# Moving the widening of weights out of the last attention slots into the first MLP

## The chip, the core and the metric

One core of a Trainium2 chip runs the whole program. Its engines are TensorE (PE, matmuls), VectorE (DVE), ScalarE (ACT), GpSimd (POOL) and SyncE (SP), which here only issues DMAs. The metric is the device time of one execution in microseconds (us), lower is better. Times inside the trace count from the first instruction.

## What is computed

Attention with random features, then an MLP block that mixes tokens and channels, then a block with a Fourier transform, a normalisation and a wider MLP. All in float32, for 4 x 576 tokens of 512 features.

```python
def _attn_ref(q, k, v, omega):
    ...
    q_p, k_p = (phi(q_s), phi(k_s))          # exp(proj - |x|^2/2 - max) / sqrt(m)
    kv = np.einsum('bhsm,bhsd->bhmd', k_p, v)
    z = np.sum(k_p, axis=2)
    num = np.einsum('bhsm,bhmd->bhsd', q_p, kv)
    den = np.einsum('bhsm,bhm->bhs', q_p, z)[..., None] + 1e-06
    return (num / den)

def _moe_ref(x, w_tok1, w_tok2, w_ch1, w_ch2):
    xt = x.transpose(0, 2, 1)
    h = np.maximum(xt @ w_tok1, 0.0) @ w_tok2
    u = x + h.transpose(0, 2, 1)
    h2 = np.maximum(u @ w_ch1, 0.0) @ w_ch2
    return (u + h2)

def _moe2_ref(x, w_ch1, w_ch2):
    ...                                       # u = x + real(fft2(x)), un = normalised u
    ch = np.maximum(un @ w_ch1, 0.0) @ w_ch2
    return (u + ch)
```

## The kernel before

Every matmul is made of three: a float32 operand is split into a high part that TensorE multiplies exactly and a low rest, and high x high, high x low and low x high are summed. The activations are split on the fly. The weights come to the core as 64-bit words and are **widened** there into a high and a low part. One chunk of weights (a slab of the first MLP, or half a pair of the second) takes one load, seven steps on VectorE, one on ScalarE and one store back to DRAM (the tile `kept`, 1 MB); when a matmul needs it, SP fetches it from there into a slot in SBUF.

The steps of a chunk of 1024 columns are, in order, with the weight that the planner gives them in us: take (L341, 0.68), ScalarE's scale (L348), rest (L352, 0.68), size (L356, 0.69), high (L360, 1.21), low (L364, 1.21), unit (L368, 0.69), scaled (L372, 1.22). After L364 the load of the chunk after next is issued (L330), after L372 the store (L406 for a slab). In attention loads and stores go through SP's queue, four steps after they fall due; from the end of attention on (`side.defer, side.queue = 0, pool`) they go through POOL's, at once.

`Side` holds the steps in one list. Its `step(budget)` is called at fixed places of the program; it adds the budget to a credit, and takes steps from the list as long as the credit covers them. So the budgets set at which place of VectorE's order a step stands, and nothing waits for a clock.

Attention runs in 72 slots and a tail of 7 (numbers n from 0 to 78). A slot projects four heads of a tile of 128 keys or queries (L506), makes its features (maximum L520, difference L527 and exponential L524 or L528), three slots later adds a key's features into the sums (L540, copied out at L545) or transposes a query's (L565), and five slots later divides (L582, L595 to L602). Keys and queries alternate; the last slot of a key is n = 60, and from there to 71 the slots are queries. Once a batch's rows are done, its token mix is put on the list `fill`, of which a slot takes about one: L667 for the hidden part, L680 for the way back, which VectorE adds into the residual (L683). Those of the last batch are still on the list when attention ends.

The first MLP (`ch_block`) runs over five blocks of the columns, the second of them short (256 columns). A block goes through the 12 slabs, the first block upwards, the second downwards. An iteration makes the hidden part of slab i (`up`, 12 matmuls, L776), takes its positive part and splits it (ScalarE L860, VectorE L861), multiplies slab i-1 down into four banks (`down`, L898), takes one item of `fill`, and calls `side.step`. The first `up` is already made in attention's tail. A slab that isn't stored yet can't be fetched: SP's instruction for it (L738) waits for the store to land, and all fetches behind it in SP's queue wait with it.

Before the change the budgets are 0 for n < 6, 1.2 up to 9, 0.45 up to 35 and 1.2 for the rest of attention, 3.9 in the first block, 1.2 in the second, and 4.3 in the others.

Of the kernel before, what the change touches and what calls it, by code (L numbers as in the profile page):

```python
# [32 lines left out]

SLOT0_US, SLOT1_US, SLOT_US, FIRST_US, SHORT_US, CH_US, FF_US, S_US, SAVED_US = 1.2, 0.45, 1.2, 3.9, 1.2, 4.3, 3.8, 1.6, 4.6


NP = NFF // 2
# [152 lines left out]
def pieces(t0, n):  # L192

    done = 0
    while done < n:
        b, s = divmod(t0 + done, S)
        step = min(n - done, S - s)
        yield done, step, b, s
        done += step
# [103 lines left out]
def mix_kernel(ctx: ExitStack, tc: tile.TileContext, qt, kt, va, om, w1, w2, wch, wff, t1, t2, out):  # L303
# [230 lines left out]
    def kv_add(i, g, part):  # L534

        off, n, b, s = part
        if s == 0:
            kvp[b, g] = bank("H")
        for hh in range(4):
            pe.matmul(out=kvp[b, g][:, hh * 65:hh * 65 + 65], lhsT=ft["k", i, g][:, hh, :],  # L540
                      rhs=src["v", i, int(off > 0)][:, 4 * g + hh, :], start=(s == 0 and hh == 0), stop=(s + n == S),
                      skip_group_check=True)
        if s + n == S:
            t = e0.tile([128, 4, D + 1], F32, tag=f"kvs{g}", name="kvs", bufs=2)
            dve.tensor_copy(out=t.rearrange("p h d -> p (h d)"), in_=kvp[b, g][:, 0:260])  # L545
            kvs[b, g] = t
            if (b, g) == (B - 1, 1):
                spare.extend("AAH")
# [12 lines left out]
    def turn(i, g):  # L561
        tp = bank("S")
        f = ft.pop(("q", i, g))
        for hh in range(4):
            pe.transpose(tp[:, hh * 128:hh * 128 + 128], f[:, hh, :], ident)  # L565
        qpt[i, g] = []
        for off, n, b, _ in pieces(i * 128, 128):
            if n < 128:
                act.copy(out=mixed_q[g][:, :, 2 * off:2 * off + n],
                         in_=tp.rearrange("p (a b) -> p a b", a=4)[:, :, off:off + n])  # L570
                t = mixed_q[g][:, :, off:off + 128]
            else:
                t = e0.tile([128, 4, 128], F32, tag="qpT", name="qpT", bufs=3)
                act.copy(out=t.rearrange("p a b -> p (a b)"), in_=tp)
            qpt[i, g].append((b, t))
# [112 lines left out]
    def last_tile(b):  # L688
        return ((b + 1) * S - 1) // 128

    order = [("k", i, g) for i in range(last_tile(0) + 1) for g in range(2)]
# [14 lines left out]
    side = Side()  # L706
# [74 lines left out]
    def attention():  # L781
        tiles = [(kind, i) for kind, i, g in order if g == (kind == "q")]
        at = {t: order.index(t + (int(t[0] == "q"),)) for t in tiles}
        late = {}
        n_all = len(order)

        def at_slot(n, kind):
            return order[n][1:] if 0 <= n < n_all and order[n][0] == kind else None

        def sums(n):  # L790
            if n in late:
                late.pop(n)()
            if (t := at_slot(n - LAG, "k")) is not None:
                parts = list(pieces(t[0] * 128, 128))
                kv_add(*t, parts[0])
                if len(parts) > 1:
                    late[n + 2] = lambda: kv_add(*t, parts[1])

        def queries(n):
            if (t := at_slot(n - LAG, "q")) is not None:  # L800
                turn(*t)
            t = at_slot(n - LAG_X, "q")
            if t is not None and t[1] == 0:
                turn_x(t[0])
                for b in range(B):
                    if t[0] == last_tile(b):
                        fill.extend(tok_mix(b))

        def results(n):
            if (t := at_slot(n - LAG_NUM, "q")) is not None:  # L810
                numer(*t)
                divide(*t)
                if t[1] == 0:
                    split_x(t[0])

        loads, splits = list(tiles), list(tiles)
        for n in range(-1, n_all + LAG_X):
            while loads and at[loads[0]] <= n + AHEAD_LOAD:
                load(*loads.pop(0))
            if n == n_all:  # L820
                enter_mlp()
            if 0 <= n < n_all:
                project(*order[n])
            sums(n)
            queries(n)
            while splits and at[splits[0]] <= n + AHEAD_SPLIT:
                split_in(*splits.pop(0))
            if 0 <= n < n_all:
                feature(*order[n])
            results(n)  # L830
            if n >= 2:

                side.step(0.0 if n < 6 else SLOT0_US if n < 10 else SLOT1_US if n < 36 else SLOT_US)
            if fill and (len(fill) > 3 or n % 2 == 0):
                fill.pop(0)()
            for fn in early[:3]:
                fn()
            del early[:3]
# [759 lines left out]
```

## Time and profile before

| | |
|---|---|
| Time, median of 3 runs | 955.7 us (954.63 to 956.05) |
| The profiled execution | 956.15 us, its span 954.1 us |
| TensorE busy | 934.5 us (98%), mean granted clock 0.996 |
| VectorE busy | 644.6 us (68%) |
| ScalarE busy | 301.5 us (32%) |
| POOL busy | 118.4 us (12%) |

Busy means that at least one instruction is under way. The granted clock is the share of TensorE's full 2.4 GHz; 0.50 is 1.2 GHz. Attention takes about the first 215 us, the first MLP's first block goes on to 291, the second block to 325.

### The profile page before, as it was taken

Reading aid. Unit: us, or ns where it says so; the run is one execution under the profiler, and the core shown is the slowest. Engines: PE = TensorE matmul, PEld = TensorE weight load, DVE = VectorE, ACT = ScalarE, POOL = GpSimd, SP = SyncE. Lnnn points to the kernel's source line nnn. Section 1 sums busy time; section 2 is a strip of 40 time slices with the busy share of each in tenths; the row PEclk is TensorE's granted clock in tenths of the full one; section 3 lists DMA queues with packets and bytes.
Section 4 is the critical chain, followed back from the end, with each engine's and each line's share of the span. In section 5 each row is a group of like instructions: output and inputs, shape, how many; then the busy total and the mean of one; then the engine's idle time right before and its main releaser. Section 6 shows DMA issues by size and latency. Waiting matters only on the chain.

```text
span 954.1 us, 14058 instructions
## 1 busy us (share of the span) xinstructions
PE 934.5 (98%) x5344; PEld 831.3 (87%) x5344; DVE 644.6 (68%) x1270; ACT 301.5 (32%) x676; POOL 118.4 (12%) x110
## 2 busy tenths in 40 slices
PE   7999999999999999999999999999999999999998
PEld 7999898888889988888888888889999998899986
DVE  5997989987776687877864577667565458533342
ACT  5886666651222222221221212222311113311121
POOL 3343333221121122011000000000000000000000
PEclk9999999899999999999999999999999999999999
DMA  7764454379999386585146438739777756787764
GB/s 267 230 198 163 147 213 167 129 300 323 348 349 424 116 325 224 193 284 194 43 179 214 161 131 272 259 113 359 268 244 242 231 183 219 227 263 256 251 208 157
DMA packets 68257, 216.47 MB, mean 227 GB/s; under 512 B 5600, under 2 KB 14432, under 8 KB 54240
## 3 DMA queue, kind: packets, MB, share of 16 engines
q1 hardware_dynamic: 60992, 172.40, 52.3%
q0 software_dynamic: 7056, 43.06, 12.3%
q8 instruction: 42, 0.69, 0.3%
q14 instruction: 23, 0.19, 0.1%
q10 hardware_dynamic: 144, 0.13, 0.0%
HBM read 169.30 MB, written 42.47 MB: 222 GB/s over the span
## 4 chain that ended last, share of the span: by engine, by line
PE 89%; DVE 8%; ACT 1%; issue 1%; DMA 0%; DVEq 0%; ACTq 0%
PE H L776 23%; PE A L898 16%; PE A L1470 14%; PE H L1457 12%; PE A L1264 7%; PE A L506 4%; PE N L582 2%; PE A L667 2%; PE H L540 2%; DVE mx L520 1%; PE S L1077 1%; DVE cvo L364 1%; PE S L1090 1%; PE S L680 1%; PE A L565 1%; DVE x L598 1%
## 5 line engine op out<-in xcount | busy, mean ns | idle before, releaser
L776 PE MATMUL H<-uh,w 128*128 128x512 f32 (+1 forms) x800 | 215.1, 354 | 1.5 <-ACT x L621 1.5
L776 PEld LDWEIGHTS H<-uh,w 128*128 128x128 f32 x800 | 136.4, 189 | 21.7 <-ACT x L621 1.7
L860 ACT ACTIVATE hh<-H 128x512 fp32r<-128x512 f32 (+1 forms) x92 | 49.0, 533 | 267.3 <-PE H L776 267.1
L776 PE MATMUL H<-ul,w 128*128 128x512 f32 (+1 forms) x304 | 113.4, 373 | 0.0
L898 PE MATMUL A<-hh,w 128*128 128x512 f32 (+1 forms) x480 | 108.7, 369 | 0.0
L1470 PE MATMUL A<-w2t,b 128*128 128x512 f32 x384 | 99.2, 394 | 0.0
L861 DVE SCALAR_TENSOR_TENSOR hl<-H,hh 128x512 fp32r<-128x512 f32 (+1 forms) x92 | 55.8, 607 | 64.0 <-ACT hh L860 63.8
L898 PEld LDWEIGHTS A<-hh,w 128*128 128x128 f32 x480 | 84.2, 188 | 15.1
L1457 PE MATMUL H<-b,w1t 128*128 128x384 f32 x480 | 91.5, 336 | 0.0
L1457 PEld LDWEIGHTS H<-b,w1t 128*128 128x128 f32 x480 | 85.0, 188 | 4.0 <-DVE tmp L1501 0.3
L1470 PEld LDWEIGHTS A<-w2t,b 128*128 128x128 f32 x384 | 70.6, 188 | 11.8
L524 ACT ACTIVATE f<-A,mx 128x128 f32<-128x128 f32 x200 | 57.5, 390 | 28.1 <-DVE mx L520 24.0
L776 PEld LDWEIGHTS H<-ul,w 128*128 128x128 f32 x304 | 57.3, 188 | 9.1
L898 PE MATMUL A<-hl,w 128*128 128x512 f32 (+1 forms) x240 | 59.2, 368 | 0.0
L1264 PE MATMUL A<-w,hh 128*128 128x512 f32 x192 | 50.5, 395 | 0.0
L520 DVE TENSOR_REDUCE mx<-A 128x4 f32<-128x512 f32 x71 | 48.2, 682 | 2.7 <-PE A L506 2.1
L898 PEld LDWEIGHTS A<-hl,w 128*128 128x128 f32 x240 | 42.6, 188 | 7.6
L364 DVE SCALAR_TENSOR_TENSOR cvo<-cvo,stg 128x1024 f32<-128x1024 int32 (+2 forms) x32 | 41.1, 1283 | 0.0
L540 PE MATMUL H<-v,f 128*128 128x65 f32 x320 | 40.1, 270 | 0.9 <-ACT f L524 0.9
L540 PEld LDWEIGHTS H<-v,f 128*128 128x128 f32 x320 | 38.9, 191 | 1.3 <-ACT f L524 1.1
L1264 PEld LDWEIGHTS A<-w,hh 128*128 128x128 f32 x192 | 34.6, 189 | 6.1
L1462 ACT ACTIVATE b<-tmp 128x384 fp32r<-128x384 f32 x16 | 8.4, 525 | 98.1 <-DVE tmp L1523 98.1
(253 smaller groups left out, 1705.1 us busy)
## 6 DMA issues: line engine op xcount, KB each, us to landing
w<-kept SPq DMA_DIRECT2D x60, 1024.0 KB, 6.9
w2t<-kept SPq DMA_DIRECT2D x55, 512.0 KB, 5.0
w1t<-kept SPq DMA_DIRECT2D x48, 512.0 KB, 4.9
stg<-in_wff_dram POOLq DMA_DIRECT2D x16, 1024.0 KB, 6.9
kept<-cvo POOLq DMA_DIRECT2D x13, 1024.0 KB, 7.4
stg<-in_wch_dram SPq DMA_DIRECT2D x9, 1024.0 KB, 6.0
kept<-cvo POOLq DMA_DIRECT2D x16, 512.0 KB, 7.6
kept<-so SPq DMA_DIRECT2D x16, 512.0 KB, 7.5
```

The costliest lines, as they stand in the source:

```text
L364: dve.scalar_tensor_tensor(out=st["l"].bitcast(F32), in0=st["l"], scalar=2.0 ** 32, in1=st["lw"].bitcast(U32), op0=ALU.mult, op1=ALU.add)
L506: pe.matmul(out=pj[:, p_ * 256:p_ * 256 + 256], lhsT=a[:, c, :], rhs=w, start=(n == 0), stop=(n == 2), skip_group_check=True)
L520: dve.tensor_reduce(out=mx, in_=p4, axis=AX.X, op=ALU.max, negate=True)
L524: act.activation(out=f[:, hh], in_=p4[:, hh], func=AF.Exp, bias=mx[:, hh])
L540: pe.matmul(out=kvp[b, g][:, hh * 65:hh * 65 + 65], lhsT=ft["k", i, g][:, hh, :], rhs=src["v", i, int(off > 0)][:, 4 * g + hh, :], start=( ...
L776: pe.matmul(out=hb[:, 0:n], lhsT=w(a, kk), rhs=u[:, kk, 0:n], start=(c == 0), stop=(c == 11))
L860: act.activation(out=hh, in_=hb[:, 0:n], func=AF.Relu)
L861: dve.scalar_tensor_tensor(out=hl, in0=hb[:, 0:n], scalar=0.0, in1=hh, op0=ALU.max, op1=ALU.subtract)
L898: pe.matmul(out=acc[i][:, 0:cols], lhsT=a[:, cs], rhs=v, start=(n == 0 and c_ == 0), stop=(n == NCH - 1 and c_ == 2))
L1264: pe.matmul(out=acc[t], lhsT=a[:, t * 128:t * 128 + 128], rhs=w, start=(n == 0 and c_ == 0), stop=(n == NFF - 1 and c_ == 2))
L1457: pe.matmul(out=to, lhsT=w[:, a, cs], rhs=v[:, q], start=(start and n == 0), stop=(n == 5), skip_group_check=True)
L1470: pe.matmul(out=acc[t], lhsT=h[n // 2][:, t * 128:t * 128 + 128], rhs=w[:, n % 2], start=(begins and n == 0), stop=(ends and n == 2))
```

## The change

Four budgets get other numbers, and a fifth is new: ALONE_US = 0.3, for the ten slots n = 58 to 67 (`alone` is the slot after the last key's, 61). The slots from 10 to 35 go from 0.45 to 0.5, the other slots from 36 on from 1.2 to 1.15. The first block's budget goes from 3.9 to 4.3, the second's from 1.2 to 1.7.

```diff
-SLOT0_US, SLOT1_US, SLOT_US, FIRST_US, SHORT_US, CH_US, FF_US, S_US, SAVED_US = 1.2, 0.45, 1.2, 3.9, 1.2, 4.3, 3.8, 1.6, 4.6
+SLOT0_US, SLOT1_US, SLOT_US, ALONE_US, FIRST_US, SHORT_US, CH_US, FF_US, S_US, SAVED_US = 1.2, 0.5, 1.15, 0.3, 4.3, 1.7, 4.3, 3.8, 1.6, 4.6
...
+        alone = max(n for n, x in enumerate(order) if x[0] == "k") + 1
...
-                side.step(0.0 if n < 6 else SLOT0_US if n < 10 else SLOT1_US if n < 36 else SLOT_US)
+                side.step(0.0 if n < 6 else SLOT0_US if n < 10 else SLOT1_US if n < 36 else
+                          ALONE_US if alone - 3 <= n < alone + 7 else SLOT_US)
```

What it moves stands in the order of the instructions on VectorE; TensorE's are in the same order as before. The lines below L835 have moved down by two in the new kernel (L861 is L863).

VectorE before, behind the last key's slot (x_1192 is a batch's residual, kvs the sums over the keys, mx and df the features' maximum and difference, rd the reciprocal in the division; cvo, cvy and stg belong to the widening):

```order
L372 SCALAR_TENSOR_TENSOR cvo<-cvo,cvy 128x1024
L352 TENSOR_SCALAR cvo<-stg 128x1024
L683 TENSOR_TENSOR x_1192<-A,x_1192 128x288
L545 COPY kvs<-H 128x260
L520 TENSOR_REDUCE mx<-A 128x4
L356 TENSOR_SCALAR cvo<-cvy 128x1024
L520 TENSOR_REDUCE mx<-A 128x4
L527 TENSOR_TENSOR df<-A,mx 128x512
```

VectorE after, at the same addition, copy and maxima (the residual is called x_1196):

```order
L683 TENSOR_TENSOR x_1196<-A,x_1196 128x288
L545 COPY kvs<-H 128x260
L520 TENSOR_REDUCE mx<-A 128x4 x2
L527 TENSOR_TENSOR df<-A,mx 128x512
L595 TENSOR_SCALAR rd<-N 128x4
L596 RECIPROCAL rd<-rd 128x4
L598 TENSOR_TENSOR x<-N,rd 128x128 x2
L602 TENSOR_TENSOR x<-N,rd 128x2
L364 SCALAR_TENSOR_TENSOR cvo<-cvo,stg 128x1024
```

The widening steps ahead of the addition and between the maxima are gone from here; the next one is a low (L364) behind a division.

VectorE before, in the first MLP block, from the second to the third of the eight additions of the last batch (x_2569 is its residual, hl the hidden part's low rest of the iteration):

```order
L683 TENSOR_TENSOR x_2569<-S,x_2569 128x288
L360 SCALAR_TENSOR_TENSOR cvo<-cvy,cvo 128x1024
L364 SCALAR_TENSOR_TENSOR cvo<-cvo,stg 128x1024
L368 TENSOR_SCALAR cvy<-cvo 128x1024
L341 TENSOR_SCALAR cvy<-stg 128x1024
L861 SCALAR_TENSOR_TENSOR hl<-H,hh 128x512
L683 TENSOR_TENSOR x_2569<-S,x_2569 128x288
L372 SCALAR_TENSOR_TENSOR cvo<-cvo,cvy 128x1024
```

VectorE after, in the same block, from the fourth to the fifth of the eight (the residual is called x_2552):

```order
L683 TENSOR_TENSOR x_2552<-S,x_2552 128x288
L352 TENSOR_SCALAR cvo<-stg 128x1024
L356 TENSOR_SCALAR cvo<-cvy 128x1024
L360 SCALAR_TENSOR_TENSOR cvo<-cvy,cvo 128x1024
L364 SCALAR_TENSOR_TENSOR cvo<-cvo,stg 128x1024
L368 TENSOR_SCALAR cvy<-cvo 128x1024
L863 SCALAR_TENSOR_TENSOR hl<-H,hh 128x512
L683 TENSOR_TENSOR x_2552<-S,x_2552 128x288
L341 TENSOR_SCALAR cvy<-stg 128x1024
L372 SCALAR_TENSOR_TENSOR cvo<-cvo,cvy 128x1024
```

The L372 that ends each of these two pieces is the last step of slab 11, the last slab of the first MLP: it stands behind the third addition before and behind the fifth after. The first MLP's block needs that slab in its twelfth iteration. Of the slabs' stores, six instead of five now go through POOL's queue in this block, and one fewer through SP's in attention.

## Rows read from the trace of the kernel before

**Rows 1.** The chain that ended last, share of the span by engine

```profile
PE 89%; DVE 8%; ACT 1%; issue 1%; DMA 0%; DVEq 0%; ACTq 0%
```

**Rows 2.** Stretches: length, busy us by engine (instructions), TensorE's granted clock, DMA

```profile
160.00:165.00 5.00, 4.22 (x36) 3.99 (x35) 4.90 (x12) 3.55 (x9) 1.34 (x2) 1.00 0.77 265
165.00:170.00 5.00, 3.01 (x24) 2.64 (x23) 5.00 (x7) 1.59 (x5) 2.17 (x1) 0.96 0.51 210
170.00:175.00 5.00, 4.70 (x22) 4.70 (x23) 4.83 (x11) 3.83 (x11) 2.37 (x1) 0.50 0.00 0
175.00:180.00 5.00, 5.00 (x40) 5.00 (x40) 4.43 (x12) 3.72 (x10) 2.57 (x2) 0.86 0.61 210
...
250.00:300.00 50.00, 50.00 (x274) 43.78 (x273) 36.47 (x53) 10.11 (x18) 9.45 (x11) 1.00 0.96 376
```

**Rows 3.** TensorE in order: start, us, instruction [idle before it and releaser]

```profile
153.27 0.36 PE L506 MATMUL A<-om_h,kh 128*128 128x256 f32 x1
...
168.14 0.54 PE L680 MATMUL A<-w2hl,h1h 128*128 128x288 f32 x2 [1.19 <-DVE x L683]
...
170.31 0.58 PE L506 MATMUL A<-om_h,qh 128*128 128x256 f32 x1 [1.10 <-ACT f L524]
```

**Rows 4.** VectorE in order, in attention, behind the last key's slot

```profile
164.00 2.04 DVE L372 SCALAR_TENSOR_TENSOR cvo<-cvo,cvy 128x1024 fp32r<-128x1024 f32 x1
165.97 1.75 DVE L352 TENSOR_SCALAR cvo<-stg 128x1024 int32<-128x1024 int32 x1
```

**Rows 5.** TensorE, first MLP block: the first matmul of up 9, 10, 11

```profile
269.68 0.39 PE L776 MATMUL H<-uh,w 128*128 128x512 f32 x1
...
275.92 0.40 PE L776 MATMUL H<-uh,w 128*128 128x512 f32 x1
...
282.17 0.39 PE L776 MATMUL H<-uh,w 128*128 128x512 f32 x1
```

**Rows 6.** VectorE in order, first MLP block

```profile
257.39 0.46 DVE L683 TENSOR_TENSOR x<-S,x 128x288 f32<-128x288 f32 x1 [1.72 <-PE S L680]
257.77 1.22 DVE L372 SCALAR_TENSOR_TENSOR cvo<-cvo,cvy 128x1024 fp32r<-128x1024 f32 x1
...
269.88 0.46 DVE L683 TENSOR_TENSOR x<-S,x 128x288 f32<-128x288 f32 x1 [1.72 <-PE S L680]
...
277.09 0.69 DVE L341 TENSOR_SCALAR cvy<-stg 128x1024 f32<-128x1024 f32 x1
```

**Rows 7.** POOL in order: stores of a slab

```profile
216.06 0.54 POOL L406 DMA_DIRECT2D kept<-cvo  x1 [0.76 <-DVE cvo L372]
...
259.28 1.03 POOL L406 DMA_DIRECT2D kept<-cvo  x1 [4.09 <-DVE cvo L372]
```

**Rows 8.** SP: a fetch, and its queue's waits from 256 to 268 (total, times, longest)

```profile
267.15 0.32 SPq L738 DMA_DIRECT2D w<-kept  x1
...
SPq L738 <- DMA kept<-cvo: 10.2, 1, 10.2
```

**Rows 9.** DMA landings (last column, us): fetches issued 211.13, 256.60, 267.15; stores 200.19, 248.00, 259.28

```profile
w<-kept SPq DMA_DIRECT2D x1, 1024.0 KB, 4.9
...
w<-kept SPq DMA_DIRECT2D x1, 1024.0 KB, 8.1
...
w<-kept SPq DMA_DIRECT2D x1, 1024.0 KB, 8.8
...
kept<-cvo SPq DMA_DIRECT2D x1, 1024.0 KB, 5.5
...
kept<-cvo POOLq DMA_DIRECT2D x1, 1024.0 KB, 6.9
...
kept<-cvo POOLq DMA_DIRECT2D x1, 1024.0 KB, 7.8
```

**Rows 10.** Second block: its last early fetch's landing, and that slab's first matmul

```profile
w<-kept SPq DMA_DIRECT2D x1, 1024.0 KB, 32.0
...
315.43 0.28 PE L776 MATMUL H<-uh,w 128*128 128x256 f32 x1
```

## The prediction

> **What bounds the kernel now.** I read the chain of waits first: 89% of the chain that ended last is TensorE and 8% VectorE [rows 1], so a change pays only where TensorE stands still, runs at its lower clock, or is made to. The table of stretches says where that is. In a stretch of 50 us from 250 on TensorE is busy for all 50 [rows 2]: after attention it never stands, and whatever delays it there is added to the time. Around the last key tile it does stand: of 5 us each it is idle for 0.78, 1.99 and 0.30 in the rows that begin at 160, 165 and 170, while VectorE is busy for 4.83 to 5.00. Its timeline names the waits: 1.19 us for the addition of a token-mix result (L683, VectorE), then 1.10 for the features (L524, which needs VectorE's maximum of L520) [rows 3]. The last projection of a key starts at 153.27 [rows 3]; from there the slots are queries alone, with less TensorE work in a slot, but a slot's share of widening is the same 1.2. VectorE's own rows there are widening steps, and two are stretched: L372 took 2.04 us and L352 took 1.75 [rows 4], where L372 takes 1.22 in the MLP [rows 6]. So VectorE sets the pace of these slots.
>
> The same rows show a second loss. After those idle stretches the granted clock fell: 0.96 of full in the row from 165, 0.50 (that is 1.2 instead of 2.4 GHz) in the row from 170, 0.86 in the row from 175. Lost to it: 5 x (0.04 + 0.50 + 0.14) = 3.4 us.
>
> **The change part by part.** TensorE's instructions stand in the same order in both kernels; only widening moves, on VectorE, with its DMAs and ScalarE's small step.
>
> *Ten slots at 0.3.* By the planner's weights the widening in slots 58 to 67 goes from 12.1 to 3.1, and the two stretched instructions leave. Slots 61 to 67 are then short of work on VectorE, not on TensorE. I book the idle time of three rows, 0.78 + 1.99 + 0.30 = 3.1 us, and the clock's 3.4 us, since the stand that came ahead of its fall is gone: **-6.5 us**. At worst the clock falls all the same or a chain from VectorE's maximum to ScalarE takes the place of the wait, and 3.1 or less is left. At best all of it goes, and that is what I book, since the chain has no third loss here that I could read. The three other slot numbers (0.45 to 0.5, 1.2 to 1.15) move 0.05 a slot: 26 slots up by 1.3 in all, 33 down by 1.7, where TensorE mostly runs; I book nothing, within 0.5 either way.
>
> *First block at 4.3, second at 1.7.* VectorE has room: in the MLP's first block an iteration lasts 6.2 us (starts at 269.68, 275.92 and 282.17 [rows 5]); one has a hidden part (L861, as many columns as L341 with its 0.69), an addition of 0.46 and widening of 3.3 to 4.5 by its weights, so 5.7 at most. The 4.4 and 5.5 more in the two blocks cost nothing by themselves as long as that room covers them.
>
> *What is late next: the slab's own way.* A slab that is widened in the block is stored by POOL, and SP's fetch waits for that store to land. With nine units less widened before the block, the rest comes later. The order on VectorE shows it for the last slab, 11: its last step L372 stood behind the third of the eight additions L683 of the last batch and now stands behind the fifth. Before: that addition at 257.39, L372 at 257.77 [rows 6], the store issued at 259.28 [rows 7], SP's fetch released by it at 267.15 after a wait of 10.2 us [rows 8], landing 8.8 us later [rows 9], at 275.95. It was needed at 282.17 [rows 5], so 6.2 us were spare (267.15 + 8.8 = 275.95). Two iterations later are 12.5 us, and the spare time is spent.
>
> After, in the times of this trace: fifth addition at 269.88 [rows 6] + 0.46, then L341 0.69 and L372 1.22 end at 272.25; the store follows 0.3 later (as 258.99 to 259.28), at 272.5. Stores beside a fetch took 6.9 and 7.8, fetches beside other transfers 8.1 and 8.8 [rows 9]. That gives 272.5 + 6.9 + 8.1 = 287.5 to 272.5 + 7.8 + 8.8 = 289.1. By the loneliest rows, a store of 5.5 and a fetch of 4.9 [rows 9], it would be 282.9. TensorE needs it at 282.17, so the stand is 5.3 to 6.9 us, and 0.7 at least. I take **+5.6 us**, near the lower row, because there is one load beside this fetch and no store until about 284, where the fetch of 8.8 had a load and two half stores beside it. Slab 10 is a smaller case of the same: its L372 now ends at 257.39 + 0.46 + 1.22 + 0.69 + 0.69 + 1.22 = 261.7, so it lands at about 277.5, 1.6 after its use at 275.92; this lies inside the 5.6, because slab 11's time doesn't depend on it. SP's queue holds the five fetches for the second block behind slab 11's. The last of them landed 32.0 us after its issue at about 270.5 and is needed at 315.43 [rows 10], 13 us later; it is moved by some 13 us, and its use by the stand: covered, with little to spare.
>
> *The clock once more.* A stand of 4 to 6 us is longer than those ahead of the fall at 170, so I expect a fall here too. The row for its price is that one fall, 3.4 us at most; part of the low stretch lies inside the stand itself and costs nothing. I take two thirds, **+2.2 us**, with 0 and 3.4 as ends.
>
> *One rule weighed.* A store's issue on POOL took 1.03 us at 259.28 and 0.54 at 216.06 [rows 7]. The Trainium skill, page "SBUF — State Buffer", section "SBUF: two separate sides", says that a DMA issued from GpSimd's queue needs its descriptors written through a port that VectorE holds during some of its instructions, so that VectorE seems to block the DMA. By that rule more widening beside the stores delays each by up to one instruction, 0.69 here, and the sum would be 0.7 higher; by the row the longer issue is already inside the 7.8, and the sum stays.
>
> *The sum.* -6.5 + 5.6 + 2.2 = +1.3 us. The profiled execution took 956.15, of which the span is 954.1; it lies 0.45 above the median of 955.7. 956.15 + 1.3 = 957.45 against that execution; against the median 957.0. So two effects of about seven microseconds cancel, and the change should not be told from none: a difference under 0.2%, 1.9 us, is about what a measurement of this kernel can't separate.
>
> **The rivals.** *Slower, by the late slab.* The store and the fetch keep slab 11's old 16.6 us (7.8 + 8.8), TensorE stands for 6.9, and the whole fall of the clock lies behind the stand: -6.5 + 6.9 + 3.4 = +3.8, 959.5. For it: these are the times that this very pair took, and five fetches queue right behind. Against: the transfers near 272 are fewer than at 267, as the block's next fetches are themselves held back. It decides from stand plus clock above 8.4 us. If moreover the waits in attention don't go (the change not doing what it says, since the features still come through ScalarE), 3 more are lost, about 962.
>
> *Faster, because the slab is hardly late.* With the lonely rows the stand is 0.7, too short to bring the clock down: -6.5 + 0.7 = -5.8, 949.9. With landings halfway (the fetch at 6, the store at 6.5) the stand is 2.9, and without a fall of the clock the time is 952.1. For it: SP issues nothing else between slab 10's fetch and slab 11's. Against: of the three fetches in rows 9 only the one at 211.13 was that quick, ahead of the block's stores, and the loads and stores of the widening go on beside this one. It decides from stand plus clock under 4.6 us.
>
> **How the numbers follow.** Forecast, both effects and nearly no difference: 0.42, 957.0. Slower by over 0.2%: 0.35, of which 0.05 is for attention not getting faster. Faster by over 0.2%: 0.23. The likeliest case's own range is 953.8 to 957.6; for 8 in 10 the range goes up to 960.5 (the slower rival with another microsecond) and down to 952.0 (landings halfway), leaving out the lone-row case and 962. Predicted: 957.0.
>
> **What would show it.** Right: between 150 and 180 VectorE well under full, TensorE without the two waits of rows 3 and the granted clock at 1.00 there, attention over some 6 us sooner; the fetch of slab 11 issued some 13 us later against the block's first matmul; a wait of L776 for a DMA (w from kept) of 4 to 7 us ahead of the last up of the first block, perhaps one under 2 ahead of the one before; a stretch of about 0.5 clock behind it. Wrong: no wait of L776 for a fetch (then store and fetch are quicker than here, and it is the faster rival), a wait without a fall of the clock (about 955), or idle time left in attention while VectorE is free (then the features' way through ScalarE was the bound). A new wait of the second block for its fetches or of VectorE for a store would put the time above the range.

## The result, and the profile after

The changed kernel took 964.5 us (median of six runs, 958.59 to 970.0) beside 955.23 us for the kernel before (six runs, 954.25 to 956.05). The ratio is 1.0097 with a 95% interval of 1.0080 to 1.0113, so it is slower by about 9 us. The prediction was 957.0, with a range of 952.0 to 960.5. The profiled execution of after took 965.94 us with a span of 964.2 us, 10.1 us more than the span before.

The chain of waits of after, its share by engine, which answers [rows 1]: TensorE still ends last nearly everywhere, but DMA has come in.

```profile
PE 88%; DVE 5%; issue 3%; DMA 3%; ACT 1%; POOL 0%; DVEq 0%; SPq 0%; ACTq 0%; POOLq 0%
```

What TensorE waited for in after, over the whole span (us in total, times, longest). The two waits of [rows 3] are gone. In their place stand two waits for kept weights, one for a copy of key-value sums (`kvs`), and two each for `df` and `x`:

```profile
PE H L776 <- DMA w<-kept: 7.9, 2, 4.8
...
PE H L540 <- DVE kvs L545: 2.0, 1, 2.0
PE A L616 <- DVE df L527: 1.5, 2, 0.8
...
PE A L565 <- DVE x L683: 1.4, 2, 1.0
```

TensorE runs the same instructions in the same order in both kernels, so each can be set beside itself. This table, worked out from the two traces, gives the start of one matmul in each and how far after lags behind.

```
matmul                           before    after     lag
key-value sums (L540)             27.75    29.29    +1.5
key-value sums (L540)             32.98    37.32    +4.3
x transposed (L616)               59.24    62.23    +3.0
x transposed (L616)              143.47   149.24    +5.8
key-value sums (L540)            146.60   153.94    +7.3
token-mix result (L680)          150.85   157.31    +6.5
query sums (L582)                176.12   175.81    -0.3
up 10, first matmul (L776)       275.92   278.45    +2.5
up 11, first matmul (L776)       282.17   289.76    +7.6
up 11, a later matmul (L776)     284.21   293.77    +9.6
```

So three things happened, and the sum is visible before any experiment. After loses 7.3 us **before** the ten slots, gains 6.8 in them (from +6.5 to -0.3), and loses 10 in the first MLP block.

**The ten slots** did what the change says. Stretches of after (length, busy us of PE, PEld, DVE, ACT and POOL with instruction counts, granted clock, DMA share and GB/s), which answer the first rows of [rows 2]; TensorE is busy but for 0.17 us and its clock stays at 1.00:

```profile
160.00:165.00 5.00, 5.00 (x45) 5.00 (x44) 3.66 (x8) 3.22 (x8) 2.07 (x2) 1.00 0.19 54
165.00:170.00 5.00, 4.83 (x42) 4.59 (x41) 4.25 (x12) 3.18 (x8) 1.16 (x1) 1.00 0.18 56
170.00:175.00 5.00, 5.00 (x46) 5.00 (x45) 4.70 (x12) 3.81 (x10) 2.87 (x3) 1.00 0.00 0
```

**The late slabs.** TensorE in order at up 10 and up 11, which answers [rows 5]: both now begin with a wait for a fetch.

```profile
278.45 0.50 PE L776 MATMUL H<-uh,w 128*128 128x512 f32 x1 [3.13 <-DMA w<-kept]
...
289.76 0.80 PE L776 MATMUL H<-uh,w 128*128 128x512 f32 x1 [4.76 <-DMA w<-kept]
```

POOL's store of slab 11 and SP's fetch of it, which answer [rows 7] and [rows 8], and the stretches around:

```profile
271.62 1.03 POOL L406 DMA_DIRECT2D kept<-cvo  x1 [3.86 <-DVE cvo L372]
```

```profile
280.97 0.32 SPq L738 DMA_DIRECT2D w<-kept  x1
```

```profile
275.00:280.00 5.00, 1.87 (x10) 1.38 (x9) 3.93 (x5) 0.00 (x0) 1.61 (x2) 1.00 0.66 259
...
285.00:290.00 5.00, 0.24 (x2) 0.24 (x2) 4.02 (x5) 0.00 (x0) 1.21 (x1) 0.70 1.04 429
290.00:295.00 5.00, 5.00 (x16) 3.99 (x17) 0.00 (x0) 0.24 (x1) 0.00 (x0) 0.62 1.01 423
```

The fetch was issued 9.35 us after the store and was there some 8.8 us later (280.97 to 289.76). The landing of the store (9.3 us from its issue) is what released it:

```profile
kept<-cvo POOLq DMA_DIRECT2D x1, 1024.0 KB, 9.3
```

Behind the stand the granted clock was 0.70 and 0.62 in two rows of 5 us, which adds the last 2 us of the lag.

**The early loss** is what the prediction didn't have. VectorE in order, after, in slot 10:

```profile
26.43 0.48 DVE L352 TENSOR_SCALAR cvo<-stg 128x640 int32<-128x640 int32 x1
28.41 0.49 DVE L356 TENSOR_SCALAR cvo<-cvy 128x640 int32<-128x640 int32 x1 [1.50 <-ACT cvy L348]
28.81 0.42 DVE L545 COPY kvs<-H 128x260 f32<-128x260 f32 x1
```

The same place before: the copy of the key-value sums comes right behind L352, and L356 three instructions later, by which time ScalarE's copy (L348, to 28.82) is just done. ScalarE's row stands last:

```profile
26.87 0.49 DVE L352 TENSOR_SCALAR cvo<-stg 128x640 int32<-128x640 int32 x1
27.27 0.43 DVE L545 COPY kvs<-H 128x260 f32<-128x260 f32 x1
27.61 0.69 DVE L520 TENSOR_REDUCE mx<-A 128x4 f32<-128x512 f32 x1
28.33 0.69 DVE L527 TENSOR_TENSOR df<-A,mx 128x512 f32<-128x512 f32 x1
28.94 0.48 DVE L356 TENSOR_SCALAR cvo<-cvy 128x640 int32<-128x640 int32 x1
```

```profile
28.07 0.75 ACT L348 ACTIVATE cvy<-cvy 128x640 f32<-128x640 f32 x1
```

With 0.5 instead of 0.45 in slot 10 the planner has just enough credit for one more step. That step, L356, needs ScalarE's scaled copy (L348), and ScalarE works it off only behind its own features. VectorE stands for 1.50 us on it; behind it in VectorE's queue is L545, which frees TensorE's accumulator. TensorE then stands for 2.02 us, and the clock falls. ScalarE's rows in after, then TensorE's, then the stretches:

```profile
26.60 1.14 ACT L524 ACTIVATE f<-A,mx 128x128 f32<-128x128 f32 x4
27.62 0.75 ACT L348 ACTIVATE cvy<-cvy 128x640 f32<-128x640 f32 x1
```

```profile
29.29 2.15 PE L540 MATMUL H<-v,f 128*128 128x65 f32 x16 [2.02 <-DVE kvs L545]
```

```profile
30.00:35.00 5.00, 5.00 (x31) 5.00 (x30) 4.56 (x8) 2.92 (x9) 0.25 (x1) 0.60 1.04 330
35.00:40.00 5.00, 5.00 (x35) 5.00 (x34) 2.44 (x4) 3.36 (x9) 1.79 (x2) 0.72 0.90 217
```

Before, both rows have a clock of 1.00:

```profile
30.00:35.00 5.00, 5.00 (x46) 4.89 (x45) 4.97 (x8) 4.06 (x14) 1.41 (x2) 1.00 1.01 344
35.00:40.00 5.00, 5.00 (x46) 5.00 (x46) 4.88 (x13) 4.35 (x14) 1.87 (x2) 1.00 1.05 271
```

A second, smaller loss of this kind lies at 148 us. VectorE, then POOL, after:

```profile
143.74 1.97 DVE L364 SCALAR_TENSOR_TENSOR cvo<-cvo,stg 128x1024 f32<-128x1024 int32 x1
145.63 1.78 DVE L368 TENSOR_SCALAR cvy<-cvo 128x1024 int32<-128x1024 int32 x1
147.33 0.45 DVE L683 TENSOR_TENSOR x<-A,x 128x288 f32<-128x288 f32 x1
```

```profile
143.32 1.30 POOL L494 TENSOR_TENSOR kl<-ks,kh 128x512 fp32r<-128x512 f32 x1 [10.17 <-ACT kh L493]
144.88 1.97 POOL L609 TENSOR_TENSOR xl<-x,xh 128x512 fp32r<-128x512 f32 x1 [0.25 <-ACT xh L608]
```

L364 and L368 take 1.22 and 0.69 in the MLP of this trace. Here each ends about 1.1 and 0.56 us after the POOL instruction beside it, so each seems to have waited for POOL first. The Trainium skill, page "SBUF — State Buffer", section "SBUF: two separate sides", says that VectorE, in some of its instructions, and GpSimd share a pair of ports that whichever starts first holds for its whole instruction while the other is blocked; these rows agree, within 0.13 us. Before, L683 stood between the two; now both are ahead of it, and TensorE waits 0.99 us for `x` (L683) and 0.76 for `df`, with the clock at 0.66 in the row from 150. Between the two places TensorE lost about another microsecond, in a wait of 1.02 us at 132 (L667) for which the profile names no releaser.

### The profile page after: what moved, and what is told of

It reads as the page before. It is cut to its first block, busy times and chain, and to the rows that moved or that the text cites. A ratio compares the mean times of both kernels' runs of the same rounds, so it can differ in the third digit from the quotient of the medians.

```text
span 964.2 us, 14070 instructions
## 1 busy us (share of the span) xinstructions
PE 936.8 (97%) x5344; PEld 835.1 (87%) x5344; DVE 642.8 (67%) x1270; ACT 302.5 (31%) x676; POOL 115.2 (12%) x112
## 4 chain that ended last, share of the span: by engine, by line
PE 88%; DVE 5%; issue 3%; DMA 3%; ACT 1%; POOL 0%; DVEq 0%; SPq 0%; ACTq 0%; POOLq 0%
PE H L776 21%; PE A L900 14%; PE A L1472 14%; PE H L1459 12%; PE A L1266 7%; PE A L506 4%; PE N L582 3%; PE H L540 2%; PE A L667 2%; PE S L1079 1%; PE A L565 1%; PE A L680 1%; DMA kept<-cvo 1%; DMA w<-kept 1%; PE S L1092 1%
## 5 line engine op out<-in xcount | busy, mean ns | idle before, releaser
L862 ACT ACTIVATE hh<-H 128x512 fp32r<-128x512 f32 (+1 forms) x92 | 49.1, 533 | 272.2 <-PE H L776 272.1
L863 DVE SCALAR_TENSOR_TENSOR hl<-H,hh 128x512 fp32r<-128x512 f32 (+1 forms) x92 | 55.8, 607 | 62.2 <-ACT hh L862 61.6
L1266 PE MATMUL A<-w,hh 128*128 128x512 f32 x192 | 50.5, 395 | 0.0
L540 PE MATMUL H<-v,f 128*128 128x65 f32 x320 | 42.0, 278 | 2.0 <-DVE kvs L545 2.0
L540 PEld LDWEIGHTS H<-v,f 128*128 128x128 f32 x320 | 41.0, 199 | 2.3 <-DVE kvs L545 2.2
L360 DVE SCALAR_TENSOR_TENSOR cvo<-cvy,cvo 128x1024 int32<-128x1024 int32 (+2 forms) x32 | 40.9, 1278 | 0.6
L1266 PEld LDWEIGHTS A<-w,hh 128*128 128x128 f32 x192 | 34.6, 189 | 6.1
```

Source lines behind the costliest of these rows:

```text
L360: dve.scalar_tensor_tensor(out=st["h"], in0=st["y"].bitcast(I32), scalar=-0x80000000, in1=st["h"], op0=ALU.bitwise_and, op1=ALU.bitwise_or)
L862: act.activation(out=hh, in_=hb[:, 0:n], func=AF.Relu)
L863: dve.scalar_tensor_tensor(out=hl, in0=hb[:, 0:n], scalar=0.0, in1=hh, op0=ALU.max, op1=ALU.subtract)
L1266: pe.matmul(out=acc[t], lhsT=a[:, t * 128:t * 128 + 128], rhs=w, start=(n == 0 and c_ == 0), stop=(n == NFF - 1 and c_ == 2))
```

## The experiments

Each kernel was timed in five rounds beside the kernel before; ratios are to that, with 95% intervals. The planner's numbers stand in one line (L36); the diffs show each as a line of its own. "Clock" is TensorE's granted clock averaged over a run's span. The 85 runs of the kernel before that were made beside these have a median of 954.5 us and a median clock of 0.998; the profiled execution of before had 0.996.

**One number alone, on the kernel before.**

```diff
-SLOT1_US = 0.45
+SLOT1_US = 0.5
```

> The kernel before with one number changed: the budget of slots 10 to 35 is 0.5 instead of 0.45. Theory A (an early stand): in slot 10 this puts a widening step (L356, which waits for ScalarE's L348) ahead of the first copy of the key sums (L545) on VectorE; VectorE idles about 1.5 us there, TensorE stands about 2 us at about 29 us, and the granted clock falls to 0.50 for 3 to 7 us: 2 to 4.5 us slower than before, 957 to 960. Theory B (all that was lost lies in the first MLP block, the early numbers move nothing): no difference, within 1 us of before, though all later steps of the widening stand a little elsewhere.

It took 962.05 us (959.05 to 964.23), ratio 1.0076 (1.0058 to 1.0095): theory A, but more than the 957 to 960 that it gave. TensorE's waits and the stretches of its profile have after's stand and after's clock:

```profile
PE H L540 <- DVE kvs L545: 2.0, 1, 2.0
```

```profile
30.00:35.00 5.00, 5.00 (x26) 5.00 (x26) 4.68 (x8) 2.92 (x9) 0.27 (x1) 0.52 1.03 332
35.00:40.00 5.00, 5.00 (x39) 5.00 (x38) 2.35 (x4) 3.32 (x9) 1.75 (x2) 0.80 0.81 183
```

So 0.05 us of planner's credit a slot, the term that the prediction booked at nothing, is enough to make the kernel before some 7 us slower. The stand at 148 us is there too (0.47 and 0.76), so it comes with 0.5 and not with 1.15. These stands are not the whole of it. The two stretched widening steps of [rows 4] have moved too: L372 (2.11 us) and L352 (1.77) now stand at 182.62 and 184.65, ahead of another maximum, and TensorE waits 2.28 us there (at 188.31). So part of what this kernel lost comes from later steps that moved.

**Slot 10 alone put back, in the kernel after.**

```diff
-side.step(0.0 if n < 6 else SLOT0_US if n < 10 else SLOT1_US if n < 36 else
+side.step(0.0 if n < 6 else SLOT0_US if n < 10 else 0.45 if n == 10 else SLOT1_US if n < 36 else
```

> The changed kernel with the budget of slot 10 alone back at 0.45; on VectorE the step L356 goes back behind the first copy of the key sums, and hardly anything else moves. Theory A: the 2 us stand at about 29 us and the clock's fall behind it go, 3 to 4.5 us less than the changed kernel, about 960 to 961; the two stands in the first MLP block stay (3 and 5 us). Theory B: as the changed kernel, 962 to 966.

960.68 us (954.97 to 963.7), ratio 1.0056 (1.0034 to 1.0077) against after's 1.0097. The wait at L540 shrank from 2.0 to 0.3 us, TensorE was not behind before up to 59 us (0.7 us ahead at 42, and 1.75 at 59, where before has a stand of 0.90), and the waits at 143 us (0.99 and 0.76) and at the slabs (1.78 and 3.35) stayed. One step in one slot is worth some 4 us, uncertain by 2.6.

**All slot numbers as before but the ten.**

```diff
-SLOT1_US, SLOT_US = 0.5, 1.15
+SLOT1_US, SLOT_US = 0.45, 1.2
```

> The changed kernel with the other slots' budgets as before (0.45 and 1.2): only the ten slots at 0.3 and the two blocks at 4.3 and 1.7 are left of the change. Theory A: no early stand, and whether there is one at 145 us depends on where a step falls beside POOL's subtraction; if both are gone, attention ends 6 to 7 us earlier than before, the late slab costs 8 to 10, and the time is 957 to 960. Theory B: the ten slots bring nothing, 962 to 966. In the profile: up 0 of the first MLP starts at 198 to 199 us (A), or at 204 to 205 (B).

954.03 us, ratio 1.0004 (0.9980 to 1.0029): no difference, where 957 to 960 was expected, and with an uncommonly wide spread of 950.43 to 961.29 in twelve runs. The profiled run is one of the good ones (span 950.1, clock 1.000), and suggests where the spread may come from; no slow run of this kernel was profiled. In it slab 11 was stored at 266.67 and fetched 5.4 us later, and up 11 waited only 0.66 us; the same two transfers took 9.35 and 8.8 us in after, which by an estimate from these rows would have been a stand of 8 here (266.67 + 9.35 + 8.8 = 284.8, needed at 276.6).

**More room in the first block, in the kernel after.**

```diff
-FIRST_US = 4.3
+FIRST_US = 4.8
```

> The changed kernel with the first block's budget at 4.8 instead of 4.3 (the credit's cap of 4.6 holds it a little lower): the last step of slab 11 stands one iteration earlier, behind the fourth addition instead of the fifth. Theory of the late slab: its store goes out 4 to 5 us earlier, TensorE's stands before up 10 and up 11 shrink from 7.9 us together to 3 to 4, and the clock's fall behind them may go: 4 to 6 us less than the changed kernel, 959 to 961. Rival (the DMA queues of this stretch are slow by themselves, whatever the order): the stands stay at 6 to 8 us, and the time too. Second rival: VectorE, with 4.6 and more of an iteration's 6.2 us, delays the hidden part and TensorE waits for L863.

961.27 us (956.54 to 963.7), ratio 1.0061 (1.0042 to 1.0081). Slab 10's wait shrank to 0.6 us. Slab 11's did not go: its store left at 268.41, some 4.5 us sooner against TensorE's work than in after, but slab 11 was there only 19.4 us behind it, and TensorE waited 4.04 us. So the stands shrank, but store and fetch took longer than in after (18.1).

**The other way: the ten slots with the old room.**

```diff
-SLOT1_US, SLOT_US, FIRST_US, SHORT_US = 0.5, 1.15, 4.3, 1.7
+SLOT1_US, SLOT_US, FIRST_US, SHORT_US = 0.45, 1.2, 3.9, 1.2
```

> The ten slots alone: slot numbers 0.45 and 1.2 and block 0's and block 1's budgets at 3.9 and 1.2 as before, so that the work left out has nowhere to go until later; slabs 10 and 11 then stand one iteration later in the order than after's for slab 10 and about the same for slab 11 (step 85), 9 also at 82. Theory (the late slabs decide): stands of 5 to 10 us at up(9) to up(11) with the clock falling behind them, median 957 to 962. If the extra room was what made slabs and stores collide: 951 to 954.

958.77 us (958.23 to 963.09), ratio 1.0049 (1.0033 to 1.0064). TensorE was 6.6 us ahead at 176 us and lost more than that in a single wait:

```profile
PE H L776 <- DMA w<-kept: 10.0, 1, 10.0
```

Slab 11's store left at 269.06 and TensorE wanted it at 277.3. So with the other slot numbers put back the slabs' lateness is enough by itself to turn the gain into a loss.

**Much more room, with the ten slots alone.**

```diff
-SLOT1_US, SLOT_US, FIRST_US, SAVED_US = 0.5, 1.15, 4.3, 4.6
+SLOT1_US, SLOT_US, FIRST_US, SAVED_US = 0.45, 1.2, 5.2, 5.6
```

> The ten slots with the other slot numbers left as before (0.45, 1.2), and block 0's budget at 5.2 us with 5.6 us that may be saved, so that the last slabs are converted about two iterations (some 12 us) earlier than with 4.3. Theory (what was left of the loss in the ten slots alone is slab 11, whose store and fetch take 11 us in its profiled run and 16 to 18 us in others): the stands of the first up-projections 10 and 11 are gone in the profiled run, the runs at 956 to 961 us are gone, and the median lies at 949 to 952, ratio to before 0.994 to 0.997. Rival 1 (VectorE or ScalarE becomes the bound of block 0, as 5.2 of its 6.2 us iteration is conversion): TensorE waits there for x or for an activation, 955 or more. Rival 2 (the 956 to 961 runs come from falls of the clock that have nothing to do with the slab): the same spread, median 953 to 955.

This missed by 15 us: 965.6 us (964.98 to 967.06), ratio 1.0116 (1.0103 to 1.0129). No fetch was waited for any more, and TensorE was 7.4 us ahead until 284 us. Then it waited for the block's own hidden part, behind widening that was waiting for DMAs. TensorE and VectorE there:

```profile
284.33 2.98 PE L900 MATMUL A<-hh,w 128*128 128x512 f32 x8 [3.20 <-ACT hh L862]
290.12 2.07 PE L900 MATMUL A<-hl,w 128*128 128x512 f32 x4 [2.81 <-DVE hl L863]
```

```profile
282.00 0.69 DVE L341 TENSOR_SCALAR cvy<-stg 128x1024 f32<-128x1024 f32 x1 [2.64 <-DMA stg<-in_wff_dram]
282.61 1.22 DVE L372 SCALAR_TENSOR_TENSOR cvo<-cvo,cvy 128x1024 fp32r<-128x1024 f32 x1
286.91 0.69 DVE L352 TENSOR_SCALAR cvo<-stg 128x1024 int32<-128x1024 int32 x1 [3.07 <-DMA kept<-cvo]
```

It is the early stand's mechanism again. With 5.2 us in every iteration the slabs are done early, the planner goes on to later matrices, and these outrun their loads and the stores that free their buffers. A widening step that waits for a DMA holds L863 behind it. The wait for `hh` is the same one engine further: ScalarE's scaling step stood for 9.18 us on VectorE's late L341, and L862, which makes `hh`, stood behind it:

```profile
282.73 1.06 ACT L348 ACTIVATE cvy<-cvy 128x1024 f32<-128x1024 f32 x1 [9.18 <-DVE cvy L341]
```

**The same room in the kernel after, and in the kernel before.**

```diff
-FIRST_US, SAVED_US = 4.3, 4.6
+FIRST_US, SAVED_US = 5.2, 5.6
```

> The kernel after, with the same room in block 0 (5.2 and 5.6), and the slot numbers 0.5 and 1.15 kept. Theory (three separate places: the early stand and the one at 148 us cost some 7, the ten slots give back 7, the late slabs cost 8 to 10 with the clock): up(10) and up(11) no longer wait, the stands at 29 and 148 us stay, and the median is 954 to 957, 8 to 10 below the kernel after. If the late slabs cost less than their stands say (the time given back later): 959 or more.

```diff
-FIRST_US, SAVED_US = 3.9, 4.6
+FIRST_US, SAVED_US = 5.2, 5.6
```

> The kernel before with block 0's budget at 5.2 and 5.6 saved and nothing else. Its slabs were in time already, so earlier ones gain nothing. Theory (room in block 0 costs nothing): 954 to 956, same as before. If the denser conversion delays block 0's own work on VectorE and ScalarE: 957 or more, with TensorE waiting in block 0.

970.66 us, ratio 1.0173 (1.0153 to 1.0193), and 971.13 us, ratio 1.0173 (1.0160 to 1.0186). Both missed for the same reason; the kernel before, whose slabs were in time, lost most beside the same kernel with less room, with 8.2 us of waits for `hl` in three places, while widening steps (L352) stood for 10.5 us on stores. All three kernels had, besides, a wait of 2.2 us for `hl` (L1266; L1264 in the kernel before) much later, with its matmul between 654 and 661 us.

**The blocks' numbers of the change alone, on the kernel before.**

```diff
-FIRST_US, SHORT_US = 3.9, 1.2
+FIRST_US, SHORT_US = 4.3, 1.7
```

> The kernel before with the two blocks' numbers of the change alone (4.3 and 1.7 in place of 3.9 and 1.2), slots untouched. Theory (room of this size in block 0 costs nothing, and slabs that were in time already gain nothing from being earlier): 954 to 956, same as before, no new wait of TensorE in block 0 or 1. If room in the blocks costs by itself, as with 5.2: 957 or more, with waits for hl behind conversions of second matrices at the end of block 0.

954.71 us (953.7 to 955.94), ratio 1.0003 (0.9995 to 1.0012), with the waits of [rows 3] in their old place and size. Room of the change's size costs nothing, and earlier slabs gain nothing, as the prediction had it. But behind those same waits the clock stayed at 1.00, where the profiled execution of before had 0.50 in the row from 170 [rows 2]; the kernel before with 5.2 had 0.66 there.

```profile
165.00:170.00 5.00, 2.70 (x23) 2.32 (x20) 4.96 (x8) 1.59 (x6) 1.84 (x1) 1.00 0.51 210
170.00:175.00 5.00, 5.00 (x44) 5.00 (x45) 4.86 (x11) 3.72 (x11) 2.36 (x1) 1.00 0.00 0
```

**Room in front.** A list in place of one number, for the ten slots with the slot numbers 0.45 and 1.2, and then for the kernel after:

```diff
-side.step(budget / 2 if twice else budget)
+side.step(budget / 2 if twice else budget[i] if isinstance(budget, list) else budget)
...
-    ch_block(0, 0, u, [lambda: (mixed(), ch_split(BLOCKS[1], u2))], FIRST_US)
+    ch_block(0, 0, u, [lambda: (mixed(), ch_split(BLOCKS[1], u2))], [5.2] * 7 + [3.0] * 4)
...
-SAVED_US = 4.6
+SAVED_US = 5.6
```

> The ten slots with slot numbers 0.45 and 1.2 as before; block 0's budget is 5.2 us in its first seven iterations and 3.0 in the last four (5.6 may be saved), so that slab 11 is converted two iterations earlier than with 4.3 throughout, and the second matrices behind it no earlier than in the kernel before. Theory (the loss with 5.2 throughout was only VectorE's queue standing behind conversions of second matrices that wait for their loads and stores in the last two iterations, and slab 11 is in time): no wait of TensorE in block 0, TensorE 6 to 7 us ahead of before at 280 us, and a median of 947 to 950, ratio 0.992 to 0.996. Rival (denser conversion in block 0 costs wherever it stands, or the falls of the clock have another cause): 953 or more.

> The kernel after with the same budget list in block 0 and its slot numbers 0.5 and 1.15. Theory (the slab's stands and the early stands add): 7 to 11 below the kernel after, and 4 to 7 above the ten slots with the same list: 953 to 957. If the numbers 0.5 and 1.15 cost nothing once the slabs are in time: as the ten slots with the list, 947 to 950.

955.86 us, ratio 1.0016 (1.0007 to 1.0024), and 963.93 us, ratio 1.0098 (1.0084 to 1.0112). Both missed, though their first MLP did as expected: in the first of them TensorE waited 1.1 us for slab 11 and nothing else, and was 6.4 us ahead at 282 us. The late wait for `hl` at L1266 was left in both:

```profile
PE A L1266 <- DVE hl L863: 2.2, 1, 2.2
```

In the first it took TensorE from 6.0 us ahead to 3.4, and lower clock behind it brought that to 1.7. Every kernel with 5.6 us to save throughout had it.

**The saving in block 0 alone.**

```diff
+    side.most = 5.6
     ch_block(0, 0, u, [lambda: (mixed(), ch_split(BLOCKS[1], u2))], [5.2] * 7 + [3.0] * 4)
+    side.most = SAVED_US
...
-SAVED_US = 5.6
+SAVED_US = 4.6
```

> As the ten slots with room in front (5.2 in seven iterations, 3.0 in four), but the 5.6 us that may be saved hold in block 0 alone; everywhere else 4.6 as before. Theory (the 2.2 us stand at 643 us behind the token mixers' steps came from the larger saving there, and cost 2.6 us and 2 us of clock behind it): no wait at the later row, TensorE 6 to 7 us ahead of before from 180 us to the end, median 949 to 952, ratio 0.994 to 0.997. If that stand has another cause: again 954 to 956 with the wait still there.

952.58 us (949.3 to 955.01), ratio 0.9980 (0.9968 to 0.9992), just above the 949 to 952 expected. The late wait is gone, so the larger saving was its cause. The profiled span is 948.3 us at a clock of 1.000, with 0.9 us of waiting for slab 11. The runs of 956 to 961 us that the ten slots had with 4.3 in the first block are gone, which fits the late slab as their cause.

The same edit on the kernel after, whose slot numbers 0.5 and 1.15 stay:

> The kernel after, all its numbers kept, with block 0's budget at 5.2 in seven iterations and 3.0 in four and 5.6 us that may be saved in block 0 alone. Theory (what the late slabs cost after is the 8 to 10 us of their stands and the clock behind them, and nothing else stands in their place): no wait for kept weights over 1.5 us, the early stand and the two at 148 us stay, the ten slots give back 7, TensorE within 1.5 us of before from 180 us to the end, median 953 to 958. Rival (the early stands cost more than the ten slots give, or the slabs' loss moves to a later place): 960 or more.

958.73 us (951.54 to 964.59), ratio 1.0040 (1.0022 to 1.0059), just above what was expected. The profiled run is a lucky one of 953.25 us, and the most telling of all. It still waits 1.7 us for slab 11, and it has the early stand of 2.0 us, but the clock stays up behind that:

```profile
PE H L540 <- DVE kvs L545: 2.0, 1, 2.0
```

```profile
30.00:35.00 5.00, 5.00 (x47) 5.00 (x46) 4.96 (x10) 3.67 (x11) 0.41 (x1) 1.00 1.03 333
35.00:40.00 5.00, 5.00 (x46) 5.00 (x46) 4.62 (x11) 5.00 (x17) 2.59 (x2) 1.00 1.00 242
```

TensorE lagged by 1.7 us at 29 us and by nothing at 59, where before has a stand of 0.90 of its own. Of the twelve runs two had a mean clock of 0.999 and 1.000 (953.25 and 951.54 us); the ten others had 0.988 to 0.994 and took 956.98 to 964.59.

**A little less cut from the ten slots, and more room in front.**

```diff
-SLOT1_US, SLOT_US, ALONE_US = 0.5, 1.15, 0.3
+SLOT1_US, SLOT_US, ALONE_US = 0.45, 1.2, 0.45
...
+    side.most = 6.0
-    ch_block(0, 0, u, [lambda: (mixed(), ch_split(BLOCKS[1], u2))], FIRST_US)
+    ch_block(0, 0, u, [lambda: (mixed(), ch_split(BLOCKS[1], u2))], [5.6] * 6 + [3.0] * 5)
+    side.most = SAVED_US
```

> The ten slots at 0.45 in place of 0.3 (1.2 before), the other slots as before, block 0 at 5.6 in six iterations and 3.0 in five, 6.0 us saved in block 0 alone: slab 11 is converted one iteration earlier than with 0.3 and 5.2. Theory (the last wait of 0.9 to 1.3 us for slab 11 goes, and the ten slots' 6 to 7 us stay since their weight steps are still a third): median 949 to 952, no wait for kept weights. Rival (more weight steps among the ten slots bring back the waits at 168 and 170 us): 952 to 955.

951.56 us (950.26 to 951.79), ratio 0.9959 (0.9947 to 0.9971): faster than both kernels. Three numbers differ from the kernel with 0.3 and the saving in block 0 alone, so which of them gave the rest isn't shown. TensorE's waits between 155 and 400 us are four, none for a fetch:

```profile
PE H L776 <- ACT x L621: 1.5, 1, 1.5
PE A L506 <- ACT f L524: 0.3, 1, 0.3
PE A L616 <- DVE x L598: 0.3, 1, 0.3
PE A L900 <- ACT hh L862: 0.2, 1, 0.2
```

Slab 11 was stored at 250.97 and its fetch issued 9.9 us later, as slowly as in after, but in time. VectorE still had two stretched steps near the ten slots (2.03 us at 157.10 and 1.78 at 178.26), and TensorE didn't wait for more than 0.3 us around them.

## Why the prediction was wrong

The change was forecast at +1.3 us and measured at +9.3. The ratios can be chained, each to the kernel before in its own rounds. From after (1.0097) to the same kernel with slabs in time (1.0040): the late slabs cost 0.57%, 5.4 us (a wait of 1.7 us for slab 11 was left). From there to the slot numbers put back (0.9980): 0.5 and 1.15 cost 0.60%, 5.7 us. From there to before: the ten slots with their slabs in time gain 0.20%, 1.9 us, and in the form with 0.45 also 0.41%, 3.9 us. The intervals make each of these uncertain by 1 to 2.5 us. The prediction had +7.8, 0 and -6.5 for the three; +5.4, +5.7 and -1.9 were measured. So the slot numbers booked at nothing and the oversized gain made the miss, and the slabs made it smaller.

- **"The three other slot numbers ... I book nothing, within 0.5 either way" is the step that failed**, by 5.7 to 7 us (from the chain, and from the kernel before with 0.5 alone), over ten times its stated bound. The argument added up credit (1.3 us in 26 slots "where TensorE mostly runs"). But the planner hands out whole steps; 0.05 more moves one step one slot forward, and what counts is which instruction then stands behind it on VectorE and what the step waits for. The order of instructions around slot 10 in after has L356 ahead of L545, and the trace of before had the price beside it: ScalarE's copy ends at 28.82 and VectorE is free for L545 at 27.27, so a step that waits for that copy there idles for some 1.55 us; it idled for 1.50. The prediction read the order only behind the last key and in the first block.
- **The ten slots: right in mechanism, oversized against the median, the second term that failed.** In the two profiled traces they give 6.8 us, for 6.5 predicted. But 3.4 of the 6.5 was the clock's fall in the profiled execution of before. That execution lost more clock than most (0.996 against 0.998; 0.4% and 0.2% of the span are 3.8 and 1.9 us), and the prediction set only 0.45 us against it. That fall is not a fixed price of these waits: with the blocks' numbers alone on the kernel before, the same waits were followed by a clock of 1.00. With the slabs in time, 1.9 to 3.9 us are left in the medians. The profiled run with 0.3 and the slabs in time (950.08) is 6.1 us below that of before (956.15), but 2.5 of it is that this run lies below its own median of 952.58, and 1.8 that the other lies above its kernel's median of those rounds, 954.36.
- **Room in the blocks costs nothing: right** for the change's 4.3 and 1.7 (ratio 1.0003), and wrong beyond. The bound that the prediction gave, 5.7 of 6.2 us busy, was not the one that came first at 5.2: later matrices' loads and stores were.
- **The late slab: right in mechanism and place, undersized in this trace.** The store was computed for 272.5, which is 271.6 in after, where the block begins 0.8 us sooner. Store and fetch took 9.35 + 8.8 = 18.1 us where 15.0 to 16.6 were taken. The fetch is the upper of its two rows; it had more company than "one load beside this fetch and no store until about 284", a half store from 279.41 and the second block's fetches from 282.01. It is the store that was undersized, 9.3 us for 6.9 to 7.8. Slab 10's fetch, itself late, ran beside it (issued at 270.91, 7.5 us), but a fetch ran beside the store of 7.8 in before too, so why it took longer stays open. So the stands were 7.9 us for the 5.6 taken and the 6.9 of the upper end. Slab 10 did wait more than foreseen (3.13 for 1.6), and, as said there, without adding to slab 11's end.
- **The clock behind it: right** in this trace, 2.0 us of lag for the 2.2 taken. In the medians stands and clock together cost less than the 7.8 booked (5.4 above). The second block's fetches, moved as foreseen, were not waited for.
- **The weighed rule** made no difference that can be seen: the store's issue took 1.03 us, as in [rows 7].
- **The rivals.** The late-slab rival named the sign, at 959.5, and the range's top of 960.5 held that case. Beyond it lay only 962, for an attention that doesn't get faster at the ten slots, and there it did. The true reason is in no rival, because every rival shared the booking of nothing.

What stays open: how large the share of the stand at 148 us is by itself, since every kernel with 0.5 in slots 11 to 35 had it, and no kernel had it alone. The nearest is the kernel after with slot 10 put back (1.0056) beside the one with all other slot numbers put back (1.0004): slots 11 to 35 and the 1.15 together cost some 5 us there, uncertain by 3.

## What to carry to other kernels

A planner's small number is not a small change: read, at each place where its steps move past another instruction, what the moved step waits for and who stands behind it on that engine, since a step that waits for another engine or a DMA stops everything queued after it. Work taken out of one stage has to be paid for at its latest use, so give the stage that takes it over its room in front, and only until the late item is done; more room than that lets later work outrun its DMAs. And before booking a recovered clock fall, see in the clock of several runs whether the profiled execution's fall is the usual one.

## What the runs showed of the hardware

The clock doesn't follow the same stand alike in every run. Behind the stand of 2.0 us at 29 us the granted clock was 0.50 to 0.60 in the next row of 5 us in four profiled kernels (after, the kernel before with 0.5 alone, after with 4.8, after with room in front), and 1.00 in two (after with 5.2 throughout, and after with its saving in block 0 alone). The twelve runs of that last kernel spread over 13 us, with mean clocks from 0.988 to 1.000. The Trainium skill, page "TensorE: Matmul & The Clock Gate", section "What's actually happening", says of a kernel's start that the number of matmuls at the lower clock varies from run to run for one and the same kernel. These runs show the like in the midst of a kernel, behind a stand. The way of a megabyte through memory and back also varied: for slab 11, from the store's issue to the fetch's, 5.4 us in the good run of the ten slots alone and 7.9 to 12.4 in the other profiled runs, whose kernels differ in a few of the planner's numbers.
